# Linear attention by another order of products: memory from the normalised input, merged into one matrix with the output weight

## The chip, the core and the metric

The kernel runs on one core of one Trainium2 chip. The metric is the device time of one execution in microseconds (us), as the median of the timed runs. The profile comes from one execution of its own. PE is the matrix engine (TensorE), PEld its weight loads, DVE VectorE, ACT ScalarE, POOL GpSimd, SP the queue that issues most transfers.

## The reference

The input has 2048 tokens of 640 features. Four residual layers follow one another, A, B, A, B; both A layers share their weights, and both B layers theirs. Each has 32 heads of 20 features.

```python
def _A_ref(x, wqkv, wo):                       # linear attention
    q, k, v = ...                              # x @ wqkv, split into heads
    phi = lambda t: jnp.where(t > 0, t + 1, jnp.exp(t)) + 1e-6
    pq, pk = phi(q), phi(k)
    kv = jnp.einsum("bhsd,bhse->bhde", pk, v)
    z = jnp.einsum("bhsd->bhd", pk)
    num = jnp.einsum("bhqd,bhde->bhqe", pq, kv)
    den = jnp.einsum("bhqd,bhd->bhq", pq, z)[..., None] + 1e-6
    return merge_heads(num / den) @ wo

def _B_ref(x, wq, wk, wv, wo, beta):           # 4 segments of 512 tokens
    # causal softmax attention in each segment, plus a read of a
    # linear memory of the segments before, mixed by a gate per head
    ...

x = x + _A_ref(_layernorm(x), A_wqkv, A_wo)
x = x + _B_ref(_layernorm(x), B_wq, B_wk, B_wv, B_wo, B_beta)
# and both once more
```

## The kernel before

**Tiles.** Tokens are handled in 4 segments of 512, each of 4 token tiles of 128; features in 5 blocks of 128 or 2 halves of 320. Weights and normalised inputs are kept as two 16-bit parts, a high and a low one, so that a product takes three 16-bit matmuls. `proj_n` (L325) makes 128 tokens by 320 outputs from 15 matmuls of 320 columns; `proj_t` (L311) makes 128 outputs by 512 tokens, transposed, from 15 of 512 columns. Every PSUM result takes one of 8 banks.

**Layer A, first pass (`a_first`).** For each segment it projects values (L325, evicted by ACT in `v_half`, L348), keys and queries (L311). phi is applied in `phi`: exponential (L337) and Relu (L339) on ACT, clamp on POOL (L341), addition on DVE (L342). Query features go to memory in `pqd` (L443). The memory of segment s is the 32-bit product of key features and values (L452), with a column of ones in each head that gives the sum z; it is added to `acc` (L460) and after the last segment masked to its heads (`masked`, L478).

**Layer A, second pass (`a_head`, `a_second`).** For each token tile `a_read` loads the query features and `read_mem` multiplies them with the memory (32-bit, L370), takes the reciprocal of the sums (L377, L378) and scales (L381). The result is transposed (`turn`, L268 to L273), multiplied with w_o (L325) and added to the input (L391). Then it is normalised and transposed for layer B. `a_head` does this for the first two tiles of a segment ahead of time, beside B's projections of the segment before.

**Layer B.** `b_project` projects a segment; `attention` runs the softmax attention of the groups of four heads (row maxima on DVE, L694; scores, L724; exponential on ACT, L728; causal mask on POOL, L735; weighted sums, L751); `b_memory` and `b_out` finish.

**The order.** PE's order is written by hand: two streams, `dense` (projections of A and B) and `attend` (attention), are interleaved by planned costs in `run`, the dense ones divided by a rate for the stage. Inside `dense`, `weave` puts steps of a second generator between those of the first: the normalisation of the next segment (`norms`), weight preparation (`w_prep`) in the opening, `a_head`, or B's output. The other engines' orders are made by a scheduler. Tiles of one tag share a fixed number of buffers: `row` 10, `pq` 5, `w` 3, `wo` 2, `big` 3. In the opening all eight weights are loaded, scaled and split (DVE L210 and L234, ACT L233); later ones are fetched by POOL's queue (L245).

## Time and profile before

| | |
|---|---|
| median of 3 runs | 1856.15 us |
| lowest, highest | 1851.01, 1856.46 us |
| profiled execution | 1850.11 us |
| its span, first to last instruction | 1848.4 us |
| mean granted clock of PE | 0.994 |
| instructions | 36154 |
| moved by DMA | 185.96 MB |

The span is what the profile's shares and slices divide. The rest of the profiled execution, 1.7 us, lies around it.

### The profile page before, as it was taken

The numbers are of one execution on the slowest core, as the hardware profiler recorded it, in microseconds if no ns is written. First come the engines' busy times: TensorE is split into PE (matmuls) and PEld (weight loads), VectorE is DVE, ScalarE is ACT, GpSimd is POOL, SyncE is SP. The second block draws the span as 40 slices with busy tenths as digits, with TensorE's granted clock in tenths as the row PEclk, the third lists the DMA queues.
The fourth block names the chain that finished last, engine by engine and source line by source line (L and its number), as shares of the span: only waits on it lengthen the run. The fifth ranks groups of instructions, "written<-read, shape, count | busy, mean of one in ns | idle before, by whom it ended". The sixth has DMA issues, their size and how long they took to land.

```text
span 1848.4 us, 36154 instructions
## 1 busy us (share of the span) xinstructions
PE 1716.3 (93%) x13032; PEld 1071.0 (58%) x13032; DVE 1144.3 (62%) x3890; ACT 911.4 (49%) x1696; POOL 503.3 (27%) x925
## 2 busy tenths in 40 slices
PE   6999999998999998898989999999989889898998
...
DVE  7655353677767686766663421527677677677883
...
GB/s 253 157 183 89 158 151 107 107 52 88 78 65 87 109 98 59 112 192 65 70 55 86 51 33 92 133 115 90 55 86 91 85 90 89 94 76 105 121 111 87
DMA packets 123307, 185.96 MB, mean 101 GB/s; under 512 B 13676, under 2 KB 85484, under 8 KB 120952
## 3 DMA queue, kind: packets, MB, share of 16 engines
...
q14 instruction: 76, 0.62, 0.1%
...
## 4 chain that ended last, share of the span: by engine, by line
PE 73%; DVE 12%; ACT 6%; issue 4%; POOL 2%; DMA 2%; SPq 1%; POOLq 0%; ACTq 0%; DVEq 0%
PE ps L325 31%; PE ps L311 18%; PE ps L751 7%; DVE junk L694 5%; PE ps L268 4%; ACT pe L728 3%; PE ps L370 3%; PE ps L724 3%; PE ps L452 2%; PE ps L687 2%; POOL e L341 1%; PE ps L582 1%; PE ps L764 1%; DVE nat L547 1%; DVE st L286 1%
## 5 line engine op out<-in xcount | busy, mean ns | idle before, releaser
L694 DVE CUSTOM_DVE_ANT_0 junk<-ps,maskw 128x512 bf16<-128x512 f32 (+3 forms) x1024 | 499.3, 488 | 83.2 <-PE ps L687 27.0
L728 ACT ACTIVATE pe<-ps,lsc 128x512 f32<-128x512 f32 x640 | 392.6, 691 | 172.6 <-PE ps L724 170.6
L735 POOL TENSOR_SCALAR_AFFINE_SELECT pe<-pe 128x256 f32<-128x256 f32 (+1 forms) x640 | 234.2, 372 | 694.4 <-ACT pe L728 689.5
L325 PEld LDWEIGHTS <-xT 128*128 128x128 f16 x2880 | 281.8, 99 | 125.4 <-issue 19.4
L325 PEld LDWEIGHTS <-oT 128*128 128x128 f16 x1920 | 186.4, 98 | 78.7 <-issue 7.6
L341 POOL TENSOR_SCALAR e<-e 128x320 f32<-128x320 f32 (+1 forms) x104 | 163.8, 1575 | 163.2 <-ACT e L337 154.4
L751 PE MATMUL ps<-pe,v 128*32 128x512 f32 (+3 forms) x2048 | 159.4, 447 | 13.5 <-ACT pe L728 6.6
L724 PE MATMUL ps<-qs,ks 62*128 62x384 f16 (+3 forms) x1024 | 131.6, 299 | 33.8 <-DVE mg L694 22.8
L325 PE MATMUL ps<-w_Bv,xT 128*128 128x320 f16 x960 | 142.4, 302 | 1.9 <-DVE mg L694 1.9
L325 PE MATMUL ps<-w_Bo,oT 128*128 128x320 f16 x960 | 141.2, 299 | 2.6 <-DVE mg L694 1.4
L325 PE MATMUL ps<-w_Av,xT 128*128 128x320 f16 x960 | 140.8, 304 | 1.6 <-DVE w_Av L234 1.0
L311 PE MATMUL ps<-xT,w_Bq 128*128 128x512 f16 x600 | 139.5, 379 | 1.5 <-DVE mg L694 0.9
L311 PE MATMUL ps<-xT,w_Bk 128*128 128x512 f16 x600 | 139.5, 379 | 0.2 <-DVE xn L391 0.2
L325 PE MATMUL ps<-w_Ao,oT 128*128 128x320 f16 x960 | 139.5, 299 | 0.0
L311 PE MATMUL ps<-xT,w_Aq 128*128 128x512 f16 x600 | 136.0, 379 | 1.3 <-DVE xT L273 0.9
L325 PE MATMUL ps<-w_Ak,xT 128*128 128x320 f16 x960 | 135.6, 299 | 1.4 <-DVE mg L694 1.4
L348 ACT ACTIVATE v<-ps 128x320 f32<-128x320 f32 x128 | 55.5, 436 | 143.4 <-PE ps L325 139.1
L291 POOL TENSOR_TENSOR rs<-rs,mhalf 128x1 f32<-128x1 f32 x64 | 35.3, 552 | 302.7 <-DVE rs L290 302.4
L751 PEld LDWEIGHTS ps<-pe,v 128*32 128x32 f32 x2048 | 66.5, 112 | 82.8 <-issue 69.3
L687 PE MATMUL ps<-ks,qs 60*128 60x512 f16 (+3 forms) x1024 | 108.4, 297 | 5.5 <-ACT pe L728 3.4
L547 DVE SCALAR_TENSOR_TENSOR nat<-ps,nat 128x512 f16<-128x512 f32 x80 | 55.3, 691 | 89.9 <-ACT nat L546 87.5
L273 DVE TENSOR_TENSOR xT<-ps,xT 128x384 f16<-128x384 f32 (+1 forms) x128 | 60.3, 484 | 78.3 <-ACT xT L272 78.1
...
## 6 DMA issues: line engine op xcount, KB each, us to landing
...
qs<-qd SPq DMA_DIRECT2D x128, 120.0 KB
ks<-kd SPq DMA_DIRECT2D x128, 120.0 KB
...
```

What stands on the lines that cost most here:

```text
L268: nc.tensor.transpose(pt[:, (c - c0) * P:(c - c0 + 1) * P], src[:, c * P:(c + 1) * P], self.ident)
L273: nc.vector.tensor_tensor(dst[:, c0:c1, 1, i * P:(i + 1) * P], v, hi, op=OP.subtract)
L311: nc.tensor.matmul(p, w[:, c, a, t * P:(t + 1) * P], xT[:, c, b, :], start=k == 0, stop=k == 3 * C - 1)
L325: nc.tensor.matmul(p, xT[:, c, a, i * P:(i + 1) * P], w[:, c, b, n * HN:(n + 1) * HN], start=k == 0, stop=k == 3 * C - 1)
L341: nc.gpsimd.tensor_scalar(e, e, 1.0, eps, op0=OP.min, op1=OP.add)
L547: nc.vector.scalar_tensor_tensor(nat[:, 1], p, QK_SHIFT, nat[:, 0], op0=OP.mult, op1=OP.subtract)
L687: nc.tensor.matmul(bs[par][:, a:a + n], qs[r, p, i * P:(i + 1) * P], ks[r, p, :n], start=True, stop=True)
L694: nc.vector.tensor_tensor_reduce(junk[:, :n], bs[par][:, a:a + n], self.maskw[:, SEG - n:], 1.0, NEG, OP.add, OP.max, G["mg"][:, par, p, i ...
L724: nc.tensor.matmul(b[:, a:a + n], ks[r, p, j * P:(j + 1) * P], qs[r, p, j * P:], start=True, stop=True)
L728: nc.scalar.activation(e, b, AF.Exp, scale=self.lsc)
L735: nc.gpsimd.affine_select(d, d, pattern=pat, compare_op=OP.is_ge, fill=0.0, base=0, channel_multiplier=-1)
L751: nc.tensor.matmul(G["pv"][32 * h4:32 * h4 + 32, j * P:], v[j][:, h * E1:h * E1 + 32], G.pop((p, par, j)), start=j == 0, stop=j == 2, skip ...
```

## The change

Layer A no longer projects values. Write x for the normalised input of the tokens, k for the key features and W for a head's columns of the value weight. The memory of a head is k^T (x W) = (x^T k)^T W. So the first pass now projects keys and queries alone and sums G = x^T k over all tokens (`memory`, 640 by 640, for all heads together), from 16-bit high and low parts of both; `norms` makes such parts of x in tokens by features (`xs`), besides the transposed ones. The sum z is kept as elementwise sums over the tiles (`L["z"]`). Queries come out as tokens by features, in halves of 320. With attention still running, keys and queries are ahead of the wait for B's values' buffers, since four of those buffers now hold G.

After the last segment, `merge` sums z over the partitions with a matrix of ones (`zb`), divides G by it, multiplies by the value weight block by block, masks to the heads and multiplies with w_o: one 640 by 640 matrix `wm`, in two 16-bit parts. The last segment's queries are fed in between its steps (`fill`). In the second pass `a_read` has no matmul: POOL multiplies the query features by z, DVE sums them over each head, takes the reciprocal and scales, and the result, transposed, is multiplied with `wm` where w_o stood. The value weight and w_o of layer A, and B's w_o, are fetched when they are needed; A's w_o comes into a key weight's buffer.

```diff
+G_ONE, P_ONE, W_SHIFT = 2.0 ** 10, 2.0 ** 14, 2.0 ** -18
...
+        self.square = cp.tile([P, P], F32, name="square")
+        nc.vector.memset(self.square, 1.0)
+        self.g_last = cp.tile([P, D], F32, name="g_last")
...
+    def ones_column(self, v):
+        self.nc.gpsimd.memset(v[:, :H * E1].rearrange("p (h e) -> p h e", e=E1)[:, :, DH:], 1.0)
...
+    def fetch_as(self, key, other):
+
+        w = self.w_tile(other)
+        self.q_w.dma_start(w, self.wd[key])
+        return w
...
+        self.k_inv = cp.tile([P, 1], F32, name="k_inv")
+        nc.vector.tensor_scalar(self.k_inv, self.inv["A", "k"], 2.0 ** 10, 2.0 ** -15, op0=OP.mult, op1=OP.max)
+        self.k_scl = cp.tile([P, 1], F32, name="k_scl")
+        nc.vector.reciprocal(self.k_scl, self.k_inv)
...
-    def phi(self, p, inv, dst, eps):
+    def phi_a(self, p, inv):
+
+        nc, sb = self.nc, self.sb
+        e = sb.tile([P, SEG], F32, tag="pq", name="e", bufs=PQ)[:, :HN]
+        nc.scalar.activation(e, p, AF.Exp, scale=inv)
+        r = sb.tile([P, 512], F32, tag="er", name="r", bufs=3)[:, :HN]
+        nc.scalar.activation(r, p, AF.Relu, scale=inv)
+        nc.gpsimd.tensor_scalar(e, e, 1.0, 1e-6, op0=OP.min, op1=OP.add)
+        nc.vector.tensor_tensor(e, e, r, op=OP.add)
+        return e
...
+        o = s % 2
+        xs = self.sb.tile([P, C, 2, D], F16, tag="wo" if o else "w", name="xs", bufs=2 if o else 3)
...
+            nc.scalar.activation(xs[:, i, 0], xh, AF.Copy)
+            nc.gpsimd.tensor_tensor(xs[:, i, 1], xh, xs[:, i, 0], op=OP.subtract)
...
+        z = self.sb.tile([P, MW], F32, tag="acc", name="z", bufs=1)
+        pqd = [self.dr.tile([NT, P, D], F32, name=f"pqd{n}_{s}") for s in range(NSEG)]
+        return dict(z=z, G=None, pqd=pqd, zb=None, wm=None)
...
+    def a_first(self, s, box, w, L, behind=None):
...
+                pk.append(sb.tile([P, 2, D], F16, tag="row", name="pk", bufs=ROWS))
...
+                    c = slice(n * HN, (n + 1) * HN)
+                    e = self.phi_a(self.proj_n(xT, w("k"), i, n), self.inv["A", "k"])
+                    nc.scalar.activation(pk[i][:, 0, c], e, AF.Copy, scale=self.k_scl)
+                    nc.vector.scalar_tensor_tensor(pk[i][:, 1, c], e, self.k_scl, pk[i][:, 0, c],
+                                                   op0=OP.mult, op1=OP.subtract)
+                    if s == 0 and i == 0:
+                        nc.vector.tensor_copy(L["z"][:, c], e)
+                    else:
+                        nc.vector.tensor_tensor(L["z"][:, c], L["z"][:, c], e, op=OP.add)
                     yield self.COST_N
...
+        def queries(i):
+            for n in range(2):
+                e = self.phi_a(self.proj_n(xT, w("q"), i, n), self.inv["A", "q"])
+                self.q_pq.dma_start(L["pqd"][s][i][:, n * HN:(n + 1) * HN], e)
+                yield self.COST_N
...
+            if s == 0:
+                L["v"] = [self.new_v(None) for _ in range(C - 1)]
+                L["G"] = [v[:, :D] for v in L["v"]] + [self.g_last]
+            for n in range(2):
+                for c in range(C):
+                    p = self.bank()[:, :HN]
+                    k = 0
+                    for i in range(NT):
+                        for a, b in ((0, 0), (0, 1), (1, 0)):
+                            nc.tensor.matmul(p, xs[:, i, a, c * P:(c + 1) * P], pk[i][:, b, n * HN:(n + 1) * HN],
+                                             start=k == 0, stop=k == 3 * NT - 1)
+                            k += 1
+                    g = L["G"][c][:, n * HN:(n + 1) * HN]
+                    if s == 0:
+                        nc.vector.tensor_copy(g, p)
+                    else:
+                        nc.vector.tensor_tensor(g, p, g, op=OP.add)
+                    yield 12 * HN * COL
...
+        yield from keys()
+        if s < NSEG - 1:
+            for i in range(NT):
+                yield from queries(i)
+            if behind:
+                yield behind
+            yield from memory()
+        else:
+            wo = self.fetch_as(("A", "o"), ("A", "k"))
+            yield from memory()
+            yield from self.merge(L, w("v"), wo, chain(*(queries(i) for i in range(NT))))
+
+    def merge(self, L, wv, wo, fill):
+
+        nc, sb = self.nc, self.sb
+
+        def filled(k):
+            for _ in range(k):
+                x = next(fill, None)
+                if x:
+                    yield x
+
+        zb = sb.tile([P, MW], F32, tag="mem", name="zb", bufs=2)
+        rz = self.row("rz")
+        for n in range(2):
+            c = slice(n * HN, (n + 1) * HN)
+            p = self.bank()[:, :HN]
+            nc.tensor.matmul(p, self.square, L["z"][:, c], start=True, stop=True)
+            nc.vector.tensor_copy(zb[:, c], p)
+            nc.vector.reciprocal(rz[:, c], zb[:, c])
+            nc.vector.tensor_scalar(rz[:, c], rz[:, c], self.k_inv, G_ONE, op0=OP.mult, op1=OP.mult)
+            yield 4 * HN * COL
+        L["zb"] = zb
+            gs.append(t)
+            for c in range(C):
+                e = sb.tile([P, SEG], F32, tag="pq", name="ge", bufs=PQ)[:, :HN]
+                nc.vector.tensor_tensor(e, L["G"][c][:, n * HN:(n + 1) * HN], rz[:, n * HN:(n + 1) * HN], op=OP.mult)
+                nc.scalar.activation(t[:, c, 0, :HN], e, AF.Copy)
+                nc.vector.tensor_tensor(t[:, c, 1, :HN], e, t[:, c, 0, :HN], op=OP.subtract)
+            yield from filled(2)
+        for v in L["v"]:
+        kt = []
+        for t in range(C):
+            p = self.bank()
+            lo, hi = LO[t] * DH, (HI[t] + 1) * DH
+            first = True
+            for n in range(2):
+                a, b = max(lo, n * HN), min(hi, (n + 1) * HN)
+                for c in range(C if a < b else 0):
+                    for k, m in ((0, 0), (0, 1), (1, 0)):
+                        nc.tensor.matmul(p[:, a - lo:b - lo], wv[:, c, k, t * P:(t + 1) * P],
...
+                        first = False
+            k2 = sb.tile([P, 2, SEG], F16, tag="pq", name="kt", bufs=PQ)
+            nc.gpsimd.memset(k2, 0.0)
+            e = sb.tile([P, 512], F32, tag="er", name="ke", bufs=3)[:, :hi - lo]
+            h = "p (h e) -> p h e"
+            nc.vector.scalar_tensor_tensor(e.rearrange(h, e=DH), p[:, :hi - lo].rearrange(h, e=DH), V_SHIFT / G_ONE,
+                                           op0=OP.mult, op1=OP.mult)
+            nc.scalar.activation(k2[:, 0, P:P + hi - lo], e, AF.Copy)
+            nc.vector.tensor_tensor(k2[:, 1, P:P + hi - lo], e, k2[:, 0, P:P + hi - lo], op=OP.subtract)
...
+            if t % 2:
+                yield from filled(1)
+        wm = sb.tile([P, C, 2, D], F16, tag="wo", name="wm", bufs=2)
+        yield from filled(1)
+        for u in range(C):
+            for n in range(2):
+                p = self.bank()[:, :HN]
+                c = slice(n * HN, (n + 1) * HN)
+                todo = [(u, slice(0, P), P)]
+                if u > 0 and (HI[u - 1] + 1) * DH > u * P:
+                    todo.append((u - 1, slice(0, 32), 32))
+                if u < C - 1 and LO[u + 1] * DH < (u + 1) * P:
...
+                for k, m in ((0, 0), (0, 1), (1, 0)):
...
+                    nc.tensor.matmul(p, kt[u][:, k, a:a + P], wo[:, u, m, c], start=k == m, stop=k == 1 and len(todo) == 1,
...
+                for k, m in ((0, 0), (0, 1), (1, 0)):
+                    for t, r, w in todo[1:]:
...
+                        nc.tensor.matmul(p[r], kt[t][:, k, a:a + w], wo[:, t, m, c], start=False, stop=k == 1,
...
+                nc.scalar.activation(wm[:, u, 0, c], p, AF.Copy, scale=W_SHIFT)
+                nc.vector.scalar_tensor_tensor(wm[:, u, 1, c], p, W_SHIFT, wm[:, u, 0, c],
...
+            yield from filled(1)
+        L["wm"] = wm
+        yield from filled(8)
...
-        pq = self.row("pqi").rearrange("p (c t) -> p c t", c=C)
-        self.q_pqi.dma_start(pq, L["pqd"][s][:, :, i * P:(i + 1) * P])
-        yield from self.read_mem([pq[:, t] for t in range(C)], L["mem"], o[i])
+        pq = self.row("pqi")
+        self.q_pqi.dma_start(pq, L["pqd"][s][i])
+        nc.gpsimd.tensor_tensor(pq, pq, L["zb"][:, :D], op=OP.mult)
+        q3 = pq.rearrange("p (h e) -> p h e", e=DH)
+        rc = self.sb.tile([P, H], F32, tag="rc", name="rca", bufs=3)
+        nc.vector.tensor_reduce(rc, q3, axis=AX.X, op=OP.add)
+        nc.vector.tensor_scalar(rc, rc, 1e-6, 1 / P_ONE, op0=OP.add, op1=OP.mult)
+        nc.vector.reciprocal(rc, rc)
+        nc.vector.tensor_tensor(q3, q3, rc[:, :, None].to_broadcast([P, H, DH]), op=OP.mult)
+        o.append(pq)
+        yield 0.0
...
+        while L["zb"] is None:
...
+        o, oT, wo = box["o"], box["oT"], L["wm"]
...
-        n = self.norms(src, 0, cur, lambda: next(v))
+        k = a("k")
...
         with self.tc.high_priority():
-            w("v")
...
             if s == 0:
-                aux = chain(a("k"), self.norms(src, 1, nxt), a("q"))
...
-                aux = chain(a("o"), self.norms(src, 2, nxt), late(), prep(("B", "v"), False))
+                aux = chain(prep(("A", "o"), False), self.norms(src, 2, nxt), late(), prep(("B", "v"), False))
...
-                aux = chain(prep(("B", "o")), last(), self.a_head(L, 0, box))
-            yield from weave(self.a_first(s, cur[0], w, L), aux, per=2)
+                self.w["A", "v"] = self.fetch(("A", "v"))
+                aux = chain(prep(("B", "o"), False), last(), self.a_head(L, 0, box))
+            yield from weave(self.a_first(s, cur, w, L), aux, per=2)
...
-        wA = {"o": self.w["A", "o"]}
-        wB = {"o": self.w["B", "o"]}
+        wA = {}
+        wB = {"o": self.fetch(("B", "o"))}
...
-                for k in "qvk":
+                for k in "kq":
...
-                yield from weave(self.a_first(2, x2[0], w, L), self.norms(src, 3, x3))
-                yield from weave(self.a_first(3, x3[0], w, L), self.a_head(L, 0, box))
+                yield from weave(self.a_first(2, x2, w, L), self.norms(src, 3, x3))
+                wA["v"] = self.fetch(("A", "v"))
...
-    nc = bacc.Bacc("TRN2", target_bir_lowering=False, num_devices=1, dynamic_dma_scratch_size=8192)
+    nc = bacc.Bacc("TRN2", target_bir_lowering=False, num_devices=1, dynamic_dma_scratch_size=4096)
```

121 lines of the change are left out of this document (47 added, 74 removed).

## The prediction

> **What bounds the kernel now.** I read the page first (busy shares, slices, chain), then the stretches of the opening and of the second projections, then the order of TensorE's work in two stages, then the groups by form.
>
> ```profile
> PE 1716.3 (93%) x13032; PEld 1071.0 (58%) x13032; DVE 1144.3 (62%) x3890; ACT 911.4 (49%) x1696; POOL 503.3 (27%) x925
> PE   6999999998999998898989999999989889898998
> DVE  7655353677767686766663421527677677677883
> PE 73%; DVE 12%; ACT 6%; issue 4%; POOL 2%; DMA 2%; SPq 1%; POOLq 0%; ACTq 0%; DVEq 0%
> ```
>
> TensorE (PE) is busy 93% of the span and carries 73% of the chain that ended last, so PE work that goes is worth up to its own time. VectorE (DVE) is second, with 12% of the chain. In the 40 slices PE is at 8 or 9 tenths nearly everywhere, while DVE is at 7 in the opening and beside attention and falls to 2 or 3 around slices 6 and 23. So the average hides three kinds of stage:
>
> ```profile
> core 0: us, PE busy (x) PEld busy (x) DVE busy (x) ACT busy (x) POOL busy (x), PEclk, DMA share, GB/s
> 20.00:80.00 60.00, 58.44 (x375) 38.76 (x374) 45.44 (x109) 35.06 (x64) 22.16 (x21) 1.00 0.53 190
> 80.00:140.00 60.00, 57.12 (x374) 38.52 (x372) 34.77 (x78) 28.91 (x53) 24.62 (x21) 0.97 0.45 167
> 140.00:200.00 60.00, 60.00 (x396) 40.23 (x395) 28.66 (x55) 30.57 (x57) 29.89 (x21) 1.00 0.29 108
> 488.00:525.00 37.00, 35.24 (x292) 25.57 (x291) 31.86 (x128) 15.41 (x28) 6.47 (x17) 1.00 0.26 84
> 696.00:832.00 136.00, 122.27 (x960) 69.26 (x959) 93.76 (x350) 73.42 (x135) 35.54 (x85) 0.97 0.38 124
> 1114.00:1171.00 57.00, 57.00 (x383) 39.46 (x382) 13.55 (x29) 17.45 (x34) 24.79 (x22) 1.00 0.25 88
> ```
>
> In the last segment of layer A's second pass through the projections (1114 to 1171) PE has no idle time and DVE is busy a quarter: PE alone sets the time. In the opening's first 60 us DVE is at 45.4 of 60, since weights are prepared there. In A's second half beside attention (488 to 525) PE has 35.2 of 37 and DVE 31.9, 86%, near the highest of any stretch: two engines are close to the limit. In B's projections (696 to 832) both have room.
>
> **The change part by part: TensorE.** The prices come from back-to-back work, start to start.
>
> ```profile
> 1104.28 9.88 PE L311 MATMUL ps<-xT,w_Aq 128*128 128x512 f16 x45
> 1113.99 16.46 PE L325 MATMUL ps<-w_Av,xT 128*128 128x320 f16 x120
> 1130.29 16.46 PE L325 MATMUL ps<-w_Ak,xT 128*128 128x320 f16 x120
> 1146.59 6.64 PE L311 MATMUL ps<-xT,w_Aq 128*128 128x512 f16 x30
> 1153.07 5.31 PE L452 MATMUL ps<-v,pk 128*128 128x147 f32 x40
> 1158.21 3.40 PE L311 MATMUL ps<-xT,w_Aq 128*128 128x512 f16 x15
> 264.72 1.62 PE L370 MATMUL ps<-mem,pqi 128*128 128x147 f32 x12
> 266.18 0.49 PE L268 MATMUL ps<-ident,oa 128*128 128x128 f32 x3
> 266.50 2.20 PE L325 MATMUL ps<-w_Ao,oT 128*128 128x320 f16 x15
> ```
>
> *Values out:* 120 matmuls of 320 columns take 1130.29 - 1113.99 = 16.30 us, 0.136 each. Eight segments (four in each of two A layers): -130.4. *Old memory out:* 1158.21 - 1153.07 = 5.14, eight times: -41.1. *G in:* 2 halves x 5 blocks x 12 matmuls of 320 columns with 128x128 16-bit weights, the same shape as the values: +130.4. *Queries:* 45 matmuls of 512 columns take 9.71 now, so the 75 of a segment 16.2; as 120 of 320 columns they take 16.3. Nothing. *Memory reads out:* one read takes 266.18 - 264.72 = 1.46, 32 of them: -46.7. So these give -41.1 - 46.7 = -87.8.
>
> *The merge in*, once per A layer: the sum over partitions is two 32-bit products of 320 columns. The old memory's 5.14 us covered 4 x 756 columns, 1.70 ns each, so 1.1 us. The product with w_v has 90 matmuls of 140 or 80 columns, 720 columns x 15 in all. At least they cost their columns (0.136/320 x 10800 = 4.6 us).
>
> ```profile
> L325 PEld LDWEIGHTS <-oT 128*128 128x128 f16 x1920 | 186.4, 98 | 78.7 <-issue 7.6 <-ACT oT L272 1.5 <-DVE oT L273 0.8
> 1172.75 0.49 PE L268 MATMUL ps<-ident,oa 128*128 128x128 f32 x3
> 1173.08 2.20 PE L325 MATMUL ps<-w_Ao,oT 128*128 128x320 f16 x15
> ```
>
> At most they cost a weight load each (98 ns, 8.8 us). Three 32-bit transposes follow one another in 1173.08 - 1172.75 = 0.33, 0.11 each, so loads overlap somewhat; I take 80 ns, 7.2 us. The product with w_o has 30 matmuls of 320 columns (4.1) and 48 narrow ones for the heads that straddle a block (6.5 at the full price, half if neighbours run together; I take the full). Sum 18.9, between 13 and 20.5; twice, +38. PE net: -87.8 + 38 = -50.
>
> **Where that does not reach the end.** *The merge's chain.* PE needs the scaled G before it can multiply by w_v. Behind the column sums stand, on DVE, two copies, two reciprocals, two scalings and 20 elementwise steps of 320 columns.
>
> ```profile
> L342 DVE TENSOR_TENSOR pk<-e,r 128x320 f32<-128x320 f32 x64 | 31.4, 491 | 98.7 <-POOL e L341 98.7
> L377 DVE TENSOR_SCALAR rc<-ps 128x16 f32<-128x16 f32 x112 | 18.3, 163 | 25.2 <-PE ps L370 24.2
> L378 DVE RECIPROCAL rc<-rc 128x16 f32<-128x16 f32 x112 | 27.7, 247 | 1.8
> L381 DVE TENSOR_TENSOR oa<-ps,rc 128x320 f32<-128x320 f32 x64 | 31.1, 486 | 1.5
> L210 DVE TENSOR_REDUCE wmx<-stage 128x1 f32<-128x640 f32 x40 | 31.1, 810 | 6.5 <-DMA stage<-in_B_wv 2.5 <-DMA stage<-in_A_wo 2.2 <-DMA stage<-in_A_wqkv 1.8
> L478 DVE TENSOR_TENSOR mem<-acc,blk 128x756 f32<-128x756 f32 x8 | 7.5, 943 | 0.2
> ```
>
> A 320-wide step is 0.49. No wide reciprocal is in the trace: its 16 columns cost 0.247 against 0.163 for a plain step, 5.3 ns a column more; so 0.49 + 1.7 = 2.2, between 0.49 and 20 x 0.247 = 4.9. [...] With 2.2, the first half of G is ready after 2 x (0.49 + 2.2 + 0.49) + 10 x 0.49 = 11.3 us, and after 13 with the query additions and head reads in between; the second about 6 later. PE has 1.1 for the sums, four query steps of 2.04 that the change places there (8.2), then two w_v blocks and another query step. It idles about 3.5 and then 1: 4.5 per merge, +9. If no query step could cover, the whole chain would show (rival one).
>
> *The reads.* They now cost POOL one 640-wide product and DVE a reduce (0.81), two small steps (0.16 and, for 32 columns, 0.33) and a 640-wide product: between 0.49 and 0.94 for 320 and 756 columns, so 0.83. That is 2.13 where two halves of (0.163 + 0.247 + 0.486) = 1.79 stood: +0.34. Two reads per layer lie in the merge and two in the first second half, where PE is full. The other twelve split: six beside B's projections (696 to 832, PE 90%, DVE 69%), where I count 80%, and six in stretches like 488 to 525. There PE falls to 32.3 and DVE rises to 32.5 of 37. At the 86% that DVE has shown, the stretch takes no less than today; at the 95% of PE there, 34.2. I count half. So six reads lose 20% (1.8) and six lose 50% (4.4), twice: 12, +1 for the rest: +13.
>
> *DVE in the opening.* A segment adds 8 low halves, 8 column sums, 8 query additions for 5 of 0.691 (row below), and 10 evictions: 34 x 0.49 - 3.5 = 13. In 20 to 80 DVE then needs 58.6 where PE needs 53.3: the 5.1 of saving there shrinks to about 1. In 80 to 140 it is 48 of 55, at the 86% mark. Four us lost. Besides, w_q now comes second, in the place of w_k:
>
> ```profile
> 21.67 6.25 PE L325 MATMUL ps<-w_Av,xT 128*128 128x320 f16 x29 [0.98 <-DVE w_Av L234]
> L234 DVE SCALAR_TENSOR_TENSOR w_Ak<-stage,scl_Ak,w_Ak x5: 876/879/880, 34.4 to 37.6; 128x640 f16<-128x640 f32 x5
> ```
>
> The second weight was ready at 38.5, and the first projection, begun near 20 and 16.3 long, now ends at about 38 with the transposes. In between DVE has the eight key halves as well, 24 x 0.49 = 11.8, so PE waits between 0 and 12 for w_q; I take 3, since weights go first in the order. +7 in all. Later segments have room (28.7 + 13 in the third of the opening's four 60 us), and the second layer A has no weights to prepare.
>
> *POOL.* The clamp of phi keeps its 320-wide price, queries become 8 instead of 5 of 512, each with a store, and each token tile adds a 640-wide subtraction.
>
> ```profile
> L342 DVE TENSOR_TENSOR pq<-e,r 128x512 f32<-128x512 f32 x40 | 27.6, 691 | 95.4 <-POOL e L341 95.4
> L341 POOL TENSOR_SCALAR e<-e 128x320 f32<-128x320 f32 x64 | 86.8, 1356 | 115.2 <-ACT e L337 108.0 <-DVE xT L273 2.1 <-DVE wm L215 1.5
> L777 POOL TENSOR_TENSOR otok<-otok,tmp 128x320 f32<-128x320 f32 x48 | 41.5, 864 | 85.5 <-DVE tmp L776 85.3
> L443 POOL DMA_DIRECT2D pqd<-pq x40 | 25.0, 624 | 46.3 <-DVE pq L342 36.4 <-DVE rc L377 4.7 <-DVE wm L220 2.0
> 180.60 1.75 POOL L341 TENSOR_SCALAR e<-e 128x320 f32<-128x320 f32 x1 [0.71 <-ACT e L337]
> L234 DVE SCALAR_TENSOR_TENSOR split<-stage,scl_Bk,split x5: 878/885/1072, 177.9 to 183.6; 128x640 f16<-128x640 f32 x5
> 222.58 1.28 POOL L341 TENSOR_SCALAR e<-e 128x320 f32<-128x320 f32 x1 [0.75 <-ACT e L337]
> ```
>
> Per segment 16 x 1.36 + 4 x 1.73 (twice the row of 320, 0.864) + 8 x 0.62 = 33.6 of some 51. Its queue has room, so the longer chain costs nothing while G's 16 us, which ask nothing of POOL, let it catch up. In the merge the five zero fills and the two w fetches behind a waiting slot hold back only reads that are not due. ScalarE swaps eight evictions of the values for eight high halves, adds four 640-wide copies a segment, and is at 35 of 60 us where it is fullest (20 to 80).
>
> ```profile
> w_Bv<-wd_Bv POOLq DMA_DIRECT2D x2, 1600.0 KB, 7.7
> ```
>
> Weight fetches grow from 9 to 13, at 7.7 us each. w_v is asked for before the last segment's keys and w_o after them, so the keys' and G's 16.3 us hide them; a late one would cost up to 7.7.
>
> **Sum.** -50 + 9 + 13 + 7 = -21 against the profiled execution's 1850.1 (span 1848.4): 1829. The three timed runs lie 1 to 6 above that execution, so I forecast **1832** for the median, against 1856.
>
> **The rivals.** *One, slower: the merge is bare.* The fill by queries needs buffers: scaled G, the masked products and query features all share five of one kind, and the five masked products stay until the end. If features cannot get one, PE waits out DVE's chain: about 19 until the second half of G is ready, then eviction of the products and of the merged weight, some 6: 25 a merge where 4.5 was counted. +41, 1873. It decides once PE idles over 15 us in a merge. For it: the first half of G alone is 11 us of DVE. Against: the query matmuls themselves need a PSUM bank only. *Two: the reads are not paid*, because DVE sets the second halves and POOL's extra 1.7 us per read delays attention's masks. The 28 that the twelve reads and those in the first second half would bring go: 1860. *Three: POOL becomes the bound of A's projections.* The same clamp takes 1.28 in a quiet stretch (222.58) and 1.75 at 180.60, while DVE splits w_Bk (177.9 to 183.6). [...] At 1.75 a query step is 1.75 + 0.62 = 2.37 on POOL against PE's 2.04, so eight query steps take 2.6 us more in each of eight segments: +21, 1853. Against: G follows, 16.3 us in which POOL catches up. *Four: PE is paid in full*, -50: 1803. That needs attention to fill what DVE leaves.
>
> **How the numbers follow.** Forecast 0.48, rival one 0.20, two 0.12, three 0.08, four 0.12. The forecast's own range is 1815 to 1850, from the bounds of merge (13 to 20.5), chain (0.49 to 4.9 a reciprocal), opening (0 to 15) and reads. The range 1796 to 1878 takes in the rivals. Faster means below 1850.6 (0.3% under 1856, about what a measurement can tell): 0.61, nearly all of the forecast, four, and a little of three. Within 0.3%: 0.11, from two and three. Slower: 0.28, all of one, the rest of two and three, and the forecast's own tail.
>
> **What would show it.** Right: PE busy near 1666, no w_Av-by-xT group, a G group of 960 matmuls at 0.136, a merge of 19 us of PE with gaps under 6, DVE busy up by some 130, the middle segments of the second A projection about 51 us each (three times 16.3 and transposes) without idle. Wrong: PE idle over 15 us in the merge, DVE at 95% in the first 120 us, the stretches like 488 to 525 still 37 us, or POOL back to back through keys and queries with PE waiting for a feature buffer.

## The result and the profile after

The changed kernel takes **1986.62 us** (median of 4 runs, 1984.14 to 1992.91); the kernel before takes 1854.88 (median of 4) beside it. The ratio is **1.072**, with an interval from 1.069 to 1.075: slower by 132 us, where 1832 was forecast. The profiled execution spans 1984.1 us.

The page of the changed kernel, in the order of the lines shown of before (busy times; 40 slices of PE, VectorE, POOL and PE's granted clock; shares of the chain that ended last):

```profile
PE 1723.9 (87%) x13032; PEld 1056.0 (53%) x13032; DVE 1298.5 (65%) x4135; ACT 963.8 (49%) x1826; POOL 636.7 (32%) x1059
PE   4867887988898898999889989899889898898998
DVE  7575656457677767767775454644767776767884
POOL 3544535102222222324444453510221232222321
PEclk9887998999999999999999999899999999999999
PE 58%; DVE 17%; POOL 9%; issue 8%; ACT 6%; DMA 2%; SPq 0%; POOLq 0%; ACTq 0%; DVEq 0%
```

PE is busy as long as before (1716.3), although memory and reads are gone, and its share of the chain fell from 73% to 58%. VectorE rose to 17% of the chain, POOL from 2% to 9%. In the first seven slices, the opening, PE is at 4 to 8 tenths, and there the granted clock is down as well. The windows of two stages (opening, middle) of the kernel before:

```profile
core 0: us, PE busy (x) PEld busy (x) DVE busy (x) ACT busy (x) POOL busy (x), PEclk, DMA share, GB/s
12.00:260.40 248.40, 241.22 (x1568) 163.91 (x1567) 136.57 (x309) 122.76 (x226) 104.48 (x88) 0.99 0.43 155
812.50:1173.10 360.60, 340.08 (x2533) 221.27 (x2532) 160.23 (x535) 162.14 (x313) 142.66 (x190) 0.99 0.23 76
```

and of the changed kernel (opening, first layer B with A's second halves, middle; the columns are the same):

```profile
12.00:340.90 328.90, 253.56 (x1723) 173.81 (x1722) 205.59 (x459) 147.09 (x290) 152.09 (x144) 0.89 0.37 134
340.90:903.50 562.60, 506.56 (x3819) 296.55 (x3817) 382.21 (x1311) 279.02 (x515) 127.51 (x278) 0.98 0.28 92
903.50:1292.50 389.00, 345.39 (x2689) 227.10 (x2688) 231.80 (x689) 187.70 (x378) 189.90 (x244) 0.96 0.23 76
```

The opening takes 80 us more for 12 us more of PE, at a mean clock of 0.89; POOL is busy 152 us there instead of 104. The middle, where layer A projects with no weights to prepare, takes 28 us more.

All runs below are cut into the same stages. The times are read from PE's timeline: *opening* from 12 us to the first product with the (merged) output weight, *B* to the last product with w_Bq in the first layer B, *middle* to the second A's first product with the output weight, *last* to PE's end.

| kernel | median or time | opening | B | middle | last |
|---|---|---|---|---|---|
| before | 1854.9 | 248 | 552 | 361 | 671 |
| before, clamp on VectorE (c1) | 1836.1 | 243 | 551 | 352 | 672 |
| changed | 1986.6 | 329 | 563 | 389 | 688 |
| changed, stores of the query features on SP's queue (e1) | 1973.0 | 310 | 575 | 378 | 693 |
| clamp on VectorE (e2) | 1902.0 | 280 | 561 | 355 | 688 |
| clamp on VectorE, no arithmetic in the reads (e8) | 1829.9 | 268 | 536 | 353 | 655 |
| clamp on VectorE, old pace of the reads (e9) | 1867.7 | 275 | 550 | 355 | 670 |
| e9, and no arithmetic in the reads (e12) | 1842.5 | 268 | 542 | 351 | 664 |

Every experiment but c2 is a single execution. The kernel before lay between 1848.1 and 1856.5 us whenever it ran, so a difference of less than about 8 us says little by itself; there the stages and the waits have to carry the reading.

### The profile page after: what moved, and what is told of

It is laid out like the page before. It is cut to its first block, busy times and chain, and to the rows that moved or that the text cites. A ratio compares the mean times of both kernels' runs of the same rounds, so it can differ in the third digit from the quotient of the medians.

```text
span 1984.1 us, 36713 instructions
## 1 busy us (share of the span) xinstructions
PE 1723.9 (87%) x13032; PEld 1056.0 (53%) x13032; DVE 1298.5 (65%) x4135; ACT 963.8 (49%) x1826; POOL 636.7 (32%) x1059
## 4 chain that ended last, share of the span: by engine, by line
PE 58%; DVE 17%; POOL 9%; issue 8%; ACT 6%; DMA 2%; SPq 0%; POOLq 0%; ACTq 0%; DVEq 0%
PE ps L347 21%; PE ps L333 12%; PE ps L881 8%; DVE junk L824 6%; POOL e L362 5%; PE ps L489 4%; PE ps L854 3%; PE ps L290 3%; ACT pe L858 2%; PE ps L817 2%; PE ps L399 2%; PE ps L712 1%; DVE e L363 1%; POOL xs L442 1%; PE ps L894 1%
## 5 line engine op out<-in xcount | busy, mean ns | idle before, releaser
L347 PEld LDWEIGHTS <-xT 128*128 128x128 f16 x2880 | 287.8, 101 | 130.1 <-issue 17.5
L362 POOL TENSOR_SCALAR e<-e 128x320 f32<-128x320 f32 x128 | 173.0, 1352 | 167.6 <-ACT e L359 163.1
L881 PE MATMUL ps<-pe,v 128*32 128x512 f32 (+3 forms) x2048 | 176.7, 477 | 11.9 <-POOL pe L865 4.6
L363 DVE TENSOR_TENSOR e<-e,r 128x320 f32<-128x320 f32 x128 | 64.5, 504 | 164.3 <-POOL e L362 163.3
L347 PE MATMUL ps<-w_Aq,xT 128*128 128x320 f16 x960 | 147.7, 313 | 1.1 <-DVE mg L824 1.1
L347 PE MATMUL ps<-wm,oT 128*128 128x320 f16 x960 | 148.4, 309 | 0.0
L347 PE MATMUL ps<-w_Ak,xT 128*128 128x320 f16 x960 | 145.7, 311 | 1.3 <-DVE mg L824 0.7
L489 PE MATMUL ps<-pk,xs 128*128 128x320 f16 x960 | 138.3, 303 | 9.8 <-ACT pk L464 7.8
L489 PEld LDWEIGHTS <-xs 128*128 128x128 f16 x960 | 94.7, 99 | 51.0 <-issue 13.9
L881 PEld LDWEIGHTS ps<-pe,v 128*32 128x32 f32 x2048 | 72.0, 117 | 89.5 <-issue 70.1
```

The lines of the kernel that those rows point to most:

```text
L347: nc.tensor.matmul(p, xT[:, c, a, i * P:(i + 1) * P], w[:, c, b, n * HN:(n + 1) * HN], start=k == 0, stop=k == 3 * C - 1)
L362: nc.gpsimd.tensor_scalar(e, e, 1.0, 1e-6, op0=OP.min, op1=OP.add)
L363: nc.vector.tensor_tensor(e, e, r, op=OP.add)
L489: nc.tensor.matmul(p, xs[:, i, a, c * P:(c + 1) * P], pk[i][:, b, n * HN:(n + 1) * HN], start=k == 0, stop=k == 3 * NT - 1)
L881: nc.tensor.matmul(G["pv"][32 * h4:32 * h4 + 32, j * P:], v[j][:, h * E1:h * E1 + 32], G.pop((p, par, j)), start=j == 0, stop=j == 2, skip ...
```

## The experiments

**First four: who holds the opening?** In the changed kernel's timeline, POOL's queue in a row of query steps (start, duration, instruction, in brackets the idle time before and what ended it):

```profile
148.37 1.27 POOL L362 TENSOR_SCALAR e<-e 128x320 f32<-128x320 f32 x1
150.47 0.61 POOL L476 DMA_DIRECT2D pqd<-e  x1 [0.82 <-DVE e L363]
151.16 1.27 POOL L362 TENSOR_SCALAR e<-e 128x320 f32<-128x320 f32 x1
```

POOL clamps (L362), waits 0.82 us until VectorE has added and its queue can issue the store, issues it in 0.61, and only then clamps again: 151.16 - 148.37 = 2.79 us a step, where PE needs 2.04. VectorE's timeline at the same place:

```profile
152.47 0.49 DVE L363 TENSOR_TENSOR e<-e,r 128x320 f32<-128x320 f32 x1 [2.30 <-POOL e L362]
152.88 0.27 DVE L226 TENSOR_REDUCE wm<-ps 1x1 f32<-1x128 f32 x1
```

and PE's:

```profile
153.21 0.58 PE L229 MATMUL ps<-wm,ones 1*128 1x1 f32 x2 [7.35 <-DVE wm L226]
```

The addition (L363) waits for POOL, the reduction for a weight's scale (L226) stands behind it in VectorE's queue though its input had long been there, and PE waits 7.35 us for that reduction (wm, on the way to a weight's scale). Theory A makes POOL's queue the cause; B says that loads of x stand behind stores of weights on SP; C that VectorE has too much work; D that the first reads are transposed too early in the merge.

e1, the store on another queue:

```diff
-QUEUES = ('gpsimd', 'scalar', 'sync', 'sync', 'gpsimd', 'sync')
+QUEUES = ('sync', 'scalar', 'sync', 'sync', 'gpsimd', 'sync')
```

> The stores of the query features go out by SP's queue and no longer by POOL's; nothing else differs from the changed kernel (1986 us). Theory A (POOL's queue paces layer A's first pass: clamp 1.27, wait 0.82 for VectorE's addition, store 0.61, so 2.79 us a query step against 2.04 of TensorE): the eight query stretches shrink to about 17 to 18 us each and the time falls by about 35, to 1950. Theory B (x loads and weight loads stand behind weight stores in SP's queue): no gain, or 5 to 15 worse, since more waiting stores now stand in that queue. Theory C (VectorE simply has too much work): within 10 of 1986.

1973.0 us. Taking only the store out of POOL's queue brings 14. By stage it is more: 30 less in the opening and the middle, where layer A projects, and 17 more in the two others, where PE's waits for the reads' loaded query features (pqi) rise from 7.4 us each to 15.0 and 11.5. But it leaves the key steps as they were, which have no store. POOL's clamps in a row of key steps of the changed kernel:

```profile
1216.00 1.28 POOL L362 TENSOR_SCALAR e<-e 128x320 f32<-128x320 f32 x1 [1.62 <-ACT e L359]
1218.89 1.28 POOL L362 TENSOR_SCALAR e<-e 128x320 f32<-128x320 f32 x1 [1.62 <-ACT e L359]
```

Here POOL waits for ACT's next exponential (L359), which stands in ACT's queue behind the copy of the last key's high half (L464), and that copy waits for VectorE's addition, so for POOL's clamp: 1218.89 - 1216.00 = 2.89 us a step by a ring of three queues. What ACT's copy waits in the whole of the changed kernel and of e2, the next run (busy, mean ns | idle before, what ended it; in e1 it is 74.1 us):

```profile
L464 ACT ACTIVATE pk<-e,k_scl 128x320 f16<-128x320 f32 x64 | 35.9, 561 | 77.1 <-DVE e L363 76.9
L463 ACT ACTIVATE pk<-e,k_scl 128x320 f16<-128x320 f32 x64 | 36.1, 564 | 22.6 <-DVE e L362 22.6
```

e2, the clamp off POOL (leaves out 1e-6 in layer A's phi):

```diff
-        nc.gpsimd.tensor_scalar(e, e, 1.0, 1e-6, op0=OP.min, op1=OP.add)
-        nc.vector.tensor_tensor(e, e, r, op=OP.add)
+        nc.vector.scalar_tensor_tensor(e, e, 1.0, r, op0=OP.min, op1=OP.add)
```

> The clamp of phi moves from POOL into VectorE's addition (one instruction, as layer B has it), so VectorE's count of instructions stays and POOL only stores; it leaves out the 1e-6 that phi adds. Theory A: key and query steps fall to TensorE's 2.04 us wherever POOL paced them; 60 us less, about 1925, and the waits of VectorE's queue for POOL are gone. Theory B: the waits for x in the opening stay at about 30 us, so no more than 20 less, 1965. Theory C: within 10 of 1986.

**1902.0 us**: 85 of the 132, more than A asked for. By stage it is 48.5 in the opening and 34 in the middle, the two places where layer A projects; B and the last layer move by 2 us or less. VectorE has no instruction more.

e3, weight stores on ACT's queue (`nc.sync.dma_start(wd, w)` becomes `nc.scalar.dma_start(wd, w)`):

> The prepared weights are written back by ScalarE's queue and no longer by SP's. Theory B: the loads of x and of the next weight no longer stand behind a store that waits for VectorE's split; TensorE's waits for the normalised input in the opening (31.6 us in the changed kernel) and for the weights' maxima (26) fall to under 15 together: 40 less, about 1945. Theory A or C: within 10 of 1986, as the normalisation waits for VectorE or POOL all the same.

1984.9: no gain; B alone is not it.

e4, the first read transposed only once the merged weight is there:

```diff
         yield from self.a_read(L, s, 1, box["o"])
+        while L["wm"] is None:
+            yield 0.0
         yield from self.turn(box["o"][0], box["oT"][0], 0)
```

> The transposes of the first tile that the second pass reads are placed on TensorE after the merged weight is done, and no longer right behind the column sums. Theory D (TensorE's fixed order meets these transposes before POOL and VectorE have made the tile, 8.7 us idle in the first merge, 5.3 in the second, at half clock for some us after): 15 to 18 less, about 1970. Rival: the read is only late because VectorE is busy with the scaled G, and the idle time moves to the products with w_v: within 5 of 1986.

1978.7, 8 less: half of what D expected. The 8.74 us for which PE stood in the first merge are gone, but it then waits 5.13 for the third read of the second half, which is not ready either.

**The control.** The same edit in the kernel before:

> The kernel before, with its clamp and addition as one instruction on VectorE as in layer B, leaving out 1e-6. Theory A (POOL's queue paced the first pass only because the change made the step of PE shorter and put a store behind it): the kernel before loses nothing to this instruction, 1855 within 5 us. Rival: the clamp on POOL cost the kernel before something too, and part of the 85 us that the clamp on VectorE brought has nothing to do with the change: 1850 or less.

1836.1 against 1853.6, one execution of each. So part of e2's gain has nothing to do with the change. Several executions of each:

> The kernel before with its clamp and addition as one instruction on VectorE, again and in rounds: the first look gave 1836.1 against 1853.6 us. If that instruction is worth it to the kernel before on its own account, 1834 to 1839 and a ratio of 0.989 to 0.992; if the first look was a chance, 1850 to 1856.

1840.1 (6 runs, 1836.91 to 1844.84) against 1851.8, ratio **0.994** from 0.992 to 0.996: faster than the kernel before by an interval that does not reach 1, though by less than the single executions said. Some 12 to 17 of the 85 us were there to be had before the change; about 70 are the change's.

**What is left in the attention stages.** Both stages of e2 are 9 and 17 us longer than before although the reads' PE work is gone. PE's waits for the row maxima, as the profile's line for all 64 such transposes of a kernel (busy, mean ns | idle before, what ended it). The kernel before:

```profile
L707 PE MATMUL pm<-ident,m 128*32 128x128 f16 x64 | 14.6, 228 | 27.2 <-DVE m L704 22.4 <-ACT r L339 2.5 <-DVE oT L273 2.0
```

The changed kernel:

```profile
L837 PE MATMUL pm<-ident,m 128*32 128x128 f16 x64 | 14.9, 232 | 50.7 <-DVE m L834 48.0 <-ACT v L377 1.3 <-DVE oT L295 0.7
```

Run e2:

```profile
L836 PE MATMUL pm<-ident,m 128*32 128x128 f16 x64 | 14.8, 231 | 48.7 <-DVE m L833 46.3 <-ACT v L376 1.3 <-DVE oT L295 0.6
```

The wait for VectorE's maxima doubled, clamp or no clamp. Theory E puts it on the reads' steps in VectorE's queue; theory F on the order: a read reported its planned cost (4 x MW columns) to the interleaving of the two streams, and reports 0 now, so attention's steps stand elsewhere.

e8, on e2:

```diff
         self.q_pqi.dma_start(pq, L["pqd"][s][i])
-        nc.gpsimd.tensor_tensor(pq, pq, L["zb"][:, :D], op=OP.mult)
...
-        nc.vector.tensor_tensor(q3, q3, rc[:, :, None].to_broadcast([P, H, DH]), op=OP.mult)
         o.append(pq)
```

> The kernel of the clamp on VectorE (1902.0 us), with the arithmetic of the read left out: the query features go to the transposes as loaded, without the product with z on POOL (1.54 us) and the sums, reciprocals and scaling on VectorE (0.82 + 0.18 + 0.35 + 0.82 = 2.17 us, 32 times). Its output is without the normalisation of layer A's read. Theory E, the reads' steps on VectorE hold back the row maxima and the transposes: PE's waits for the row maxima and for pqi in the two stages of attention (PE idle 52.9 and 66.8 us, before 35.3 and 47.1) return to those of before, 37 us less, and some 10 of PE at half clock behind those waits: 1850 to 1865. Theory F, the waits come from another order of the streams (the read no longer counts in the pace of the dense stream, so attention's steps stand elsewhere): the waits for the row maxima stay within 5 us of what they were and only the waits for pqi go (about 8 in the merges, 10 in the second halves): 1880 to 1890. If neither is right: 1900.

1829.9, 72 less, beyond both totals. The waits are what theory E asked for: PE idles 36.3 and 48.0 us in the two attention stages, and the wait for the row maxima is back near that of before, though the order is e2's:

```profile
L829 PE MATMUL pm<-ident,m 128*32 128x128 f16 x64 | 14.5, 227 | 32.8 <-DVE m L826 25.3 <-DVE oT L295 5.1 <-ACT v L376 1.7
```

e9, on e2, no instruction added or taken away:

```diff
         o.append(pq)
-        yield 0.0
+        for _ in range(2):
+            yield 2 * MW * COL
```

> The kernel of the clamp on VectorE (1902.0 us), where each read reports to the interleaving of the two streams the cost that the old read had (two steps of 2 x MW columns), so that attention's steps stand between the tiles of the second halves as in the kernel before; no instruction is added or taken away. Theory F, order: PE's waits for the row maxima fall from 21 us in each attention stage towards 9 to 12, total 1880 to 1890. Theory E, VectorE's queue: the waits stay, total within 5 us of 1902.

**1867.7**, 34 less and more than F asked for. The group of the row maxima in e9:

```profile
L837 PE MATMUL pm<-ident,m 128*32 128x128 f16 x64 | 14.8, 231 | 27.4 <-DVE m L834 23.9 <-ACT r L371 1.5 <-DVE oT L295 1.0
```

It is back near the 22.4 of before, and the second halves beside attention take 35.3 and 34.5 us as in the kernel before (35.3 and 35.3), where e2's took 41.5 and 38.9. So the order alone undoes the wait, as F says, and so does leaving out the reads' arithmetic in the new order (e8, 25.3): it takes both, the reads' steps and the places that the planned cost of 0 gave to attention's steps. E and F are halves of one cause. The same edit alone, with the clamp on POOL:

> The changed kernel (1986.6 us, clamp on POOL) with nothing but the reads' pace: each read reports to the interleaving the cost of the old read. With the clamp on VectorE that brought 34 us, 29 of them in the two attention stages. Theory F, order: the same attention stages gain the same, 1950 to 1960, the opening stays at 325 to 330. Theory A2, the clamp on POOL disturbs attention's order as well, and the two gains overlap: 1965 or more.

1957.5, 29 less, so the two prices nearly add up (85 + 29 against 85 + 34).

e12, e9 with e8's edit:

> The kernel of the clamp on VectorE with the reads' pace (1867.7 us), with the arithmetic of the reads left out as in the run without it (product with z on POOL; sums, reciprocals and scaling on VectorE). It prices that arithmetic once attention's steps stand where they stood. Theory E, VectorE's queue still holds back the transposes and row maxima: the 46.7 us of PE that the reads no longer need appear in the two attention stages (549.5 and 670.1 fall to 526 to 532 and 646 to 652), the merges lose their waits of 6.4 and 3.3: 1812 to 1825. Theory F, order was all: only the waits for pqi go (9.7 in the merges, about 8 in each attention stage): 1838 to 1846.

1842.5, what F expected: 25 less. PE's waits for the reads (17.1 us for pqi and 6.4 for the first read's sums in e9) are gone. With the arithmetic gone, the old pace is the worse one by 13 us (e8): the best pace depends on what a read costs VectorE and POOL, and the planner knows only PE's columns.

e13, on e9, the read's last scaling on POOL (`nc.gpsimd.tensor_tensor`):

> The kernel of the clamp on VectorE with the reads' pace (1867.7 us), with the last step of the read, the scaling of q by the reciprocal sums (0.82 us on VectorE, 32 times), on POOL, where the product with z takes 1.54 us. Theory E, VectorE's queue is what costs: 26 us of it are gone, row maxima and transposes come earlier, 1855 to 1862. Theory H, the length of the read's own chain costs (each transposed tile waits for its read, and POOL's step is longer by 0.7 us): 1868 to 1880.

1866.3: neither. In the restored order, 26 us of VectorE's work moved without effect, which leaves the time from the load of pq to the scaled tile as what the reads cost in the right order; that part is argued from PE's waits for pqi, not shown by a run of its own.

**The opening.** In e9 it is still 32 us longer than in c1 (24 in e12). Windows of e9 (the columns as above):

```profile
22.00:50.00 28.00, 18.89 (x115) 12.37 (x114) 25.76 (x55) 18.71 (x37) 4.94 (x4) 0.88 0.66 240
75.00:100.00 25.00, 25.00 (x185) 17.93 (x184) 16.65 (x37) 8.38 (x16) 0.00 (x0) 1.00 0.44 146
100.00:125.00 25.00, 19.02 (x122) 13.43 (x121) 20.71 (x50) 18.09 (x37) 8.65 (x10) 0.86 0.48 178
```

and of c1:

```profile
22.00:50.00 28.00, 27.84 (x194) 19.65 (x192) 24.79 (x61) 16.55 (x35) 2.19 (x4) 1.00 0.71 259
75.00:100.00 25.00, 25.00 (x172) 16.69 (x170) 12.39 (x24) 11.63 (x23) 1.67 (x3) 1.00 0.43 155
100.00:125.00 25.00, 24.63 (x166) 16.55 (x164) 16.53 (x35) 15.61 (x31) 1.14 (x2) 1.00 0.43 157
```

Between 22 and 50 and between 100 and 125, key steps with a weight in preparation, VectorE is at 25.8 of 28 and 20.7 of 25 and PE stands; in the G and query steps (75 to 100) PE is full. In c1 part of these steps project values, which ACT evicts; yet VectorE is at 24.8 of 28 there in the first window too, and PE hardly stands, so VectorE's share alone proves nothing. Summed over PE's timeline, e9 waits 21.0 us for xh, the normalised input (1.9 for the first segment's, then 6.9, 6.0 and 5.8 at the three changes of segment), c1 only the 1.9. Seven runs tried to take that away.

e7, on e2, z added up on POOL (`nc.gpsimd` for the copy and the addition to z):

> The kernel of the clamp on VectorE (1902.0 us), and in addition the running sum z of the key features on POOL instead of VectorE: 8 additions of 0.48 us per segment, 3.9 us, leave VectorE's queue; POOL, which the clamp has left, does them. Opening of the kernel before 248.4 us, of the clamp on VectorE 280.4. Theory C, VectorE has too much work in the opening (the next segment's x is normalised late because its statistics stand behind z, pk and the weights' low halves): the three waits of PE for the next segment's xh (6.9, 6.0 and 5.8 us) fall by 2 to 4 each, the opening by 8 to 14, total 1888 to 1894. Theory C2, the wait is for something else in the opening (loads, ACT): waits and total as they were, 1902 within 4. Theory P, POOL's queue is again the pace (an addition of 320 columns by about 0.8 to 1.5 us, and POOL also subtracts for xs and takes the power for the statistics): total up by 5 or more.

1906.9, the waits for xh 20.8; the opening falls by 4 us and the other stages rise by 9. VectorE was hardly lighter: in the opening it is busy 199.8 us against e2's 204.5, where the 30 additions had taken 14.6, and its timeline and POOL's show why. VectorE:

```profile
97.62 0.54 DVE L464 SCALAR_TENSOR_TENSOR pk<-e,k_scl,pk 128x320 f16<-128x320 f32 x1
99.28 0.88 DVE L240 SCALAR_TENSOR_TENSOR split<-stage,scl_Ao,split 128x640 f16<-128x640 f32 x1
100.07 1.15 DVE L464 SCALAR_TENSOR_TENSOR pk<-e,k_scl,pk 128x320 f16<-128x320 f32 x1
```

POOL:

```profile
96.14 0.87 POOL L469 TENSOR_TENSOR z<-z,e 128x320 f32<-128x320 f32 x1 [1.61 <-DVE e L362]
99.50 1.37 POOL L469 TENSOR_TENSOR z<-z,e 128x320 f32<-128x320 f32 x1 [2.49 <-DVE e L362]
```

The subtraction for pk takes 0.54 alone and 1.15 where an addition on POOL, begun at 99.50, ends at 100.87; that one takes 1.37 instead of 0.87.

e10, on e9, more rows (`ROWS = 12`, `PE_BUFS = 9`):

> The kernel of the clamp on VectorE with the reads' pace (1867.7 us), with 12 row buffers instead of 10 (and 9 instead of 10 buffers for attention's exponentials, which make the room; those are in use after the opening only). Opening 275.2 us there, 243.2 in the kernel before with the clamp on VectorE; PE waits 21.0 us in it for the next segment's xh, because x of that segment is issued only behind the store of the weight in preparation (three of its four loads at 103.39, behind the store at 102.97), where the kernel before had issued it some 40 us earlier. Theory R, the rows: the keys pk now hold their four row buffers until the product G at the end of the segment, so x finds no buffer: with two more, the loads come earlier, the waits for xh fall below 8 us, the opening to 252 to 262, total 1847 to 1856. Theory C, VectorE's order: the statistics of x stand behind the weight's low halves and phi whenever x comes: opening within 4 us of 275, total 1864 to 1872. In both, one buffer less for the exponentials may cost up to 5 us in the attention stages (549.5 and 670.1).

1902.7. The opening is 275.3 as before, and three of x's four loads are still issued right behind the weight's store (103.00, the store at 102.58): R falls. The 35 us more lie in the attention stages and the middle (559.5, 362.4, 687.5), where one buffer less for the exponentials and the rows differ. No run separates the two, but the trace points to the exponentials: ACT's exponential now waits 34.0 us for the weighted sums (L881), which free its buffers, and no such wait is among e9's three largest.

```profile
L858 ACT ACTIVATE pe<-ps,lsc 128x512 f32<-128x512 f32 x640 | 400.2, 692 | 215.6 <-PE ps L854 165.9 <-PE ps L881 34.0 <-DVE rc L407 13.7
```

e11, e3's edit on e9:

> The kernel of the clamp on VectorE with the reads' pace (1867.7 us), with the stores of the prepared weights on ACT's queue instead of SP's, so that no load of x on SP stands behind a store that waits for VectorE's low halves (18 us at 102.97). With the clamp on POOL this brought nothing (1984.9 against 1986.6), but POOL's queue then held the opening. Theory B, SP's queue: with POOL out of the way the waits for xh fall from 21 us to 10 or less, total 1850 to 1858. Theories R and C: no load moves, or it does and VectorE is late all the same: 1864 to 1872. ACT waits for VectorE at each of these stores, which may hold its evictions: 5 us up at most.

1873.7, opening 281.7. The loads of x did come early, as SP's timeline shows, and it did not help:

```profile
86.10 4.51 SPq L301 DMA_DIRECT2D x<-in_A_x  x4
```

VectorE's timeline:

```profile
105.24 0.88 DVE L240 SCALAR_TENSOR_TENSOR split<-stage,scl_Ao,split 128x640 f16<-128x640 f32 x1
107.83 0.88 DVE L308 BATCH_NORM_STATS2 st<-x 128x6 f32<-128x320 f32 x2
```

All four tiles of x were asked for by 90.6, but their statistics (L308) start at 107.83, behind the last low half of the weight (L240) and the keys in VectorE's queue.

e14, on e9, the loads and statistics ahead of the weight's preparation:

```diff
-                aux = chain(a("q"), self.norms(src, 1, nxt), prep(("A", "v"), False))
+                ahead = self.norms(src, 1, nxt)
+                next(ahead)
+                aux = chain(a("q"), ahead, prep(("A", "v"), False))
...
-                aux = chain(prep(("A", "o"), False), self.norms(src, 2, nxt), late(), prep(("B", "v"), False))
+                ahead = self.norms(src, 2, nxt)
+                next(ahead)
+                aux = chain(prep(("A", "o"), False), ahead, late(), begin(), prep(("B", "v"), False))
```

> The kernel of the clamp on VectorE with the reads' pace (1867.7 us), with the loads and statistics of the next segment's x put into the program ahead of the preparation of the weight that shares the segment with them (segments 1 and 2; for segment 3 ahead of the preparation of layer B's value weight); no instruction is added. Three runs have taken away one thing each, and the waits for xh stayed at 21 us: more rows (x still behind the store on SP), the stores on ACT (x there at 86 to 90 us, but its statistics behind the weight's low halves on VectorE until 107.8), z on POOL. Theory S, both queues in series: x is behind the weight's store on SP and its statistics behind the weight's low halves on VectorE, so only taking both away helps: waits for xh below 6 us, opening 275.2 to 248 to 256, with PE no longer at half clock behind them, total 1840 to 1850. Theory C, VectorE simply has too much work in the opening (205 us of 329 in the changed kernel): then the waits move to the weights and keys, opening 268 or more, total 1860 to 1868.

1876.9, opening 282.3. The waits for xh fell to 13.2, those for the weights' scales rose from 4.2 to 13.2, and 3.3 for a tile's statistics (mv) came in. That spoke for C.

e17, on e9, no running additions to z:

> The kernel of the clamp on VectorE with the reads' pace (1867.7 us), with the running additions to z left out (all but the first copy): the normaliser is then wrong, and each key step has 0.49 us less on VectorE, with nothing given to POOL in its place (z on POOL made VectorE's subtractions for pk 1.15 us long where they met it, and 0.55 elsewhere, so that run did not lighten VectorE). Opening 275.2 us, waits for xh 21.0; VectorE is busy 25.8 of 28 us between 22 and 50, and 20.7 of 25 between 100 and 125, where PE stands. Theory C, VectorE's work in the key stretches is the bound: 3.9 us less in each of them, the three waits fall by 2 to 4 us each, opening 262 to 268, total 1852 to 1860. Theory D, the order in which VectorE meets its work and not the amount: waits within 3 us of 21, total 1863 to 1870.

1867.9: waits 19.3. Theory C, as an amount of work on VectorE, falls. The window from 98 to 107 us in e9:

```profile
98.00:107.00 9.00, 5.08 (x38) 3.42 (x35) 8.90 (x19) 6.62 (x13) 0.00 (x0) 1.00 0.42 159
```

and in e17:

```profile
98.00:107.00 9.00, 7.09 (x53) 4.89 (x50) 8.37 (x17) 8.62 (x17) 0.00 (x0) 1.00 0.11 46
```

With VectorE relieved (8.37 for 8.90), ACT filled up, 8.62 of 9 us. PE did more in this window too, as its wait begins some 2 us later than in e9.

e18, on e9, the norms of segments 2 and 3 first, the weights after:

> The kernel of the clamp on VectorE with the reads' pace (1867.7 us), with the norms of segments 2 and 3 put ahead of the preparation of weights in their segment, and their loads and statistics ahead of the preparation that ends the segment before (segment 1 as it was). The weight's low halves then fall into the query and G stretches, where VectorE has room (16.7 of 25 us busy between 75 and 100). Theory C, work of VectorE in the key stretches: the waits for xh of segments 2 and 3 (6.0 and 5.8 us, each followed by PE at half clock) go and do not come back elsewhere; the first (6.9) stays; opening 260 to 266, total 1850 to 1858. Rival: as in the run with the norms ahead in all segments, the waits move to the weights: opening 275 to 283, total 1866 to 1877.

1873.1, opening 281.7: waits for xh 16.5, for the weights' scales 12.5: the rival.

e20, on e17, without the keys' Relu on ACT as well:

> The kernel without the running additions to z (1867.9 us), with the positive part of the keys' features left out as well: one ACT instruction of 0.52 us less per key step of layer A, the same number on VectorE; normaliser and keys are then wrong. In the run without z PE still waited 19.3 us for xh in the opening (275.2 us, 243.2 in the kernel before with the clamp on VectorE): between 98 and 107 us ACT was busy 8.62 of 9 and VectorE 8.37, where with z it was VectorE 8.90 and ACT 6.62. Theory CA, the key stretch gives both ACT and VectorE about as much as PE's step of 2.04 us holds once a weight is prepared beside it, so that either alone can be lightened without gain: with both lighter the three waits for xh fall to 10 us or less in sum, opening 258 to 266, total 1848 to 1858. Theory D, the latency of the chain of statistics and the order of the queues, not the amount of work: waits 16 to 20, opening 271 or more, total 1863 to 1868.

1860.4, opening 271.4, waits 17.7, between the two theories and nearer to D. The same window:

```profile
98.00:107.00 9.00, 4.42 (x31) 3.14 (x30) 5.96 (x14) 5.19 (x11) 0.56 (x1) 0.88 0.59 202
```

Here VectorE was busy 5.96 of 9 and ACT 5.19, and PE still stood for half of it, from 101.8 to 106.4, in which VectorE was busy for 2.2 us.

**Where the three waits end.** Each ends with the first tile of a segment, and in e9 the x of that tile had been asked for long before (at 29.43, 83.35 and 139.43 us), not behind the weight's store; its statistics stand in VectorE's order until 43.55, 105.05 and 156.13. The second wait, which ends at 109.1, in the timelines of SP and VectorE:

```profile
83.35 0.43 SPq L301 DMA_DIRECT2D x<-in_A_x  x1
105.05 0.48 DVE L308 BATCH_NORM_STATS2 st<-x 128x6 f32<-128x320 f32 x1
```

So e10 and e11, which aimed at the loads, could not take these waits away; e14, which moved the statistics, cut them to about 3 us each and paid in the weights' scales.

**What stays open.** Neither more rows, nor either queue alone, nor VectorE's or ACT's amount of work, nor two other orders bring the opening under 271 us while c1 has 243. What the runs leave is the order and latency of three queues together (keys, weight, statistics), each step of which was moved only at the cost of another. A version with the values' place kept, so that weights are prepared beside steps that ask nothing of VectorE, was not tried.

## Why the prediction was wrong

**Mechanism, PE's count: right, and not paid.** G is 960 matmuls at 0.144 us (138.3 in all; 0.136 was taken), the merge 21.7 us of PE in the changed kernel and 19.1 in e2 (18.9 was taken). Yet PE busy is 1723.9 where 1666 was expected, for the same matmuls ran longer. The rows of before were 159.4 (L751), 139.5 (w_Ao) and 135.6 (w_Ak); now:

```profile
L881 PE MATMUL ps<-pe,v 128*32 128x512 f32 (+3 forms) x2048 | 176.7, 477 | 11.9 <-POOL pe L865 4.6 <-ACT pe L858 4.4 <-ACT r L361 1.0
L347 PE MATMUL ps<-wm,oT 128*128 128x320 f16 x960 | 148.4, 309 | 0.0
L347 PE MATMUL ps<-w_Ak,xT 128*128 128x320 f16 x960 | 145.7, 311 | 1.3 <-DVE mg L824 0.7 <-DVE w_Ak L240 0.5
L347 PE MATMUL ps<-w_Aq,xT 128*128 128x320 f16 x960 | 147.7, 313 | 1.1 <-DVE mg L824 1.1
```

17 + 9 + 10 us, and 12 for the queries, which have the keys' 960 matmuls and should cost their 135.6: 48 of the 58 missing. The granted clock has it: 0.959 in the mean, where the kernel before had 0.994. By the clock's records it is halved in 33 stretches after the first 12 us, 164 us in all (7 and 24 us in the kernel before), and over nine tenths of the time that the matmuls of these four groups took beyond their medians lies where it is down. Shortly ahead of each stretch PE had waited 1.8 us or longer. A run of 32 weighted sums of attention in the kernel before, from PE's timeline:

```profile
510.87 2.35 PE L751 MATMUL ps<-pe,v 128*32 128x512 f32 x32
```

and at the same place of the changed kernel (granted clock 0.50 from 603.88 to 607.88):

```profile
603.87 0.29 PE L837 MATMUL pm<-ident,m 128*32 128x128 f16 x1 [3.59 <-DVE m L834]
603.88 4.55 PE L881 MATMUL ps<-pe,v 128*32 128x512 f32 x32
```

**The failed step: POOL's term, set to zero.** "Its queue has room, so the longer chain costs nothing" compared 33.6 us of POOL's work with 51 us of a segment. The work was right (152 us in the opening, with the statistics, the merge's fills and the first reads) but the queue does not run at its busy time. A query step also waits 0.82 us for VectorE's addition before the store, and holds VectorE's queue in turn: 2.79 us against PE's 2.04. A key step closes the ring over ACT, 2.89 us; its link is the high half of the key in ACT's queue, which the prediction counted as work, in exchange for the values' evictions, and not as a wait. e2 prices both at 85 us, of which about 70 are the change's. Rival three named the place, at 1853 and 0.08, but not the mechanism: its 2.37 a step is a clamp slowed to 1.75 and a store, where the clamp took 1.35 in the mean and the waits are what counts; and its "POOL catches up" in G did not help PE, which had waited in the keys and queries already. For the same reason the sign that was given, POOL back to back, is not what the trace shows: POOL waits in each of the steps shown.

**The reads** (13 us lost of 46.7): 34 for their planned cost, which the prediction never asked after, and 25 for their own chain (72 where the pace stays as changed, so the two overlap). Rival two had the place right (the second halves grew to 41.5 and 38.9 us, from 35.3) and half of the cause: the reads' steps do hold attention back (e8), but only in the order that the planned cost of 0 made (e9), which it did not name. **The merge's chain** (4.5 us of idle PE each): 9.0 in the second merge and 12.5 in the opening's, 8.74 of it for the reads' transposes put into PE's order early, and only 3.7 for the masked products. The scaled G was in time. Its reciprocal was sized well, 2.12 us where 2.2 was taken:

```profile
L528 DVE RECIPROCAL rz<-zb 128x320 f32<-128x320 f32 x4 | 8.3, 2120 | 0.0
```

**VectorE in the opening** (7 us): 32 remain in e9 against c1, 8 of them for the first reads; this term was an amount of work, and e17 and e20 show that less work on VectorE, or on ACT too, does not bring the time back. Rivals one and four did not come about; no merge had 15 us of idle time.
